# An attention and gated-FFN kernel: its four PSUM pairs addressed as eight banks, and a new written order

## The chip, the core and the metric

The kernel runs on one core of a Trainium2 chip. The metric is the device time of one execution in microseconds (us); lower is better. The kernel before was timed three times: 277.92, 278.68 and 278.79 us, median 278.68 us. Differences of about 0.3% (0.8 us) and more can be told from none.

## What is computed

Block-sparse attention (4 batches, 8 heads, 768 tokens, head size 64), and a gated feed-forward network on its output. The mask lets a block of 32 queries see its neighbour blocks, the first and last block, and three drawn blocks.

```
scores = scale * np.matmul(q, k.transpose(0, 1, 3, 2))
scores = np.where(mask, scores, -1e9);  attn = softmax(scores);  a = attn @ v
x = a.transpose(0, 2, 1, 3).reshape(3072, 512)
gate = 1 / (1 + exp(-(x @ w_gate)));  out = (gate * (x @ w_val)) @ w_out        # d_ff = 1536
```

Inputs and output are float32; the kernel computes in float16 with float32 accumulation.

## The kernel before

**Tiling.** The 3072 tokens are cut into twelve units of 256 queries, three per batch (n = 0 to 11). A unit has four pairs of heads (p = 0 to 3). For each pair there are three steps (j = 0 to 2) of 256 keys: a step's score matmuls (qk) fill a [128, 1024] float32 result in PSUM, ACT takes the exponential into SBUF as float16 (exp), and DVE multiplies it by the 0/1 mask (mul; unit 0 has the mask added in the score matmuls instead, as a bias). Then the value product (pv), its normalisation on DVE (norm: a reciprocal and a multiply; from unit 2 on a fold of two partial sums comes first), and a transpose of the result into xT: by TensorE for units 0 and 1 (turn, and a copy), by a transposing DMA after them. The FFN of a unit or of two units then runs over twelve tiles of 128 hidden columns (f0 to f11): gate and value matmuls, tanh on ACT (it stands for the sigmoid), gate on DVE, and the output product y. A job takes two f tiles for a single unit (units 0 to 3), one for two units.

**Start.** The first heads come in float32 by the hardware queues. All else is loaded by POOL's queue, with a cast to float16, in the order of `FIRST`: k, q for the first unit by pairs (k1 q1 k2 q2 k3 q3), v0 to v3, then the rest of q by pairs (r0 to r3) between the weight tiles w0 to w5 (two f tiles each), then the output weights. K and q of batch 0 are transposed by TensorE (prep); later batches by DMA.

**PSUM.** All of PSUM is four tiles of two banks each, `m0` to `m3` (line 317). Every job takes one such pair whole, also those that need one bank or less: turn, the transposes of prep, the mask tiles, the value product of units 0 and 1.

**The written order.** Each job is a task with a number (`Plan.add`, line 133). The string `ORDER` names the tasks in the order in which they are issued, with the engine (D for DVE, A for ACT) where there is a choice, the pair after a colon, and after an @ a task that must be done before a load goes out. `Plan.run` (line 137) walks the string and calls the tasks. Each engine has one queue and takes its instructions in that order; where an instruction reads or overwrites what another engine's instruction, named earlier in the string, wrote or read, the tile layer adds a semaphore wait to it. A waiting instruction holds everything behind it on its engine.

**Junk.** Tokens that begin with j issue matmuls on zeros into a pair, in front of the first real work on TensorE.

Of the kernel before, what the change touches and what calls it, by code (L numbers as in the profile page):

```python
# [22 lines left out]
NT = S // 128  # L23
# [8 lines left out]
PE, ACT, DVE, DMA, SP = "PADGS"  # L32
# [4 lines left out]
EARLY = 2  # L37
# [3 lines left out]
j3 j3 j3 j3 j3 j3 j3 j3 5A 8D j3 0 11A j3s 9:0 j3s j3s j3s 10D j3s j3s 12:1 1:2 j3s 13A 3:0 2 j3s 34:1 4D 35 15:2  # L41
j3s 32:3 16D 6:0 33 17:1 7D 117:2 18D 97:0 118D 44:1 98A j3s 22:3 78:2 23D 45 36:0 79D 20:3 37 21D
40:2 25:1 30:3 41 26D 76:0 77D 46:1 31 54:2 19 74:0 47 75D 27:3 24 55 50:0 28D 80:1 64:3 51 81D
48:2 65 60:1 49 56:0 61 14 66:3 58:2 67D 105@30 57 29 89:3 59 38:1 90 52:0 86:2 53D 87 39 68:3
93:0 69D 62:1 108:2 94 42:3 109 43D 102:0 63D 111:3 70:1 103 110 126:2 71D 112 104 95:0 84:1 96D
122:3 85A 113 140:0 127 123 91 130:1 128 132:3 141 129 131 72:2 119:0 99:1 73D 133 120 147:2 134
100 135 142 157:0 148 154:3 171:1 124 155 149 158 88 164:3 143:2 156 176:0 92@164 144 121 146@111
101 172 170@44 165 173 161:2 217@54 145 190:1 177 189@46 162 125@40 178 237@54 159 186:3 191 150:2
115:0 151D 192 174:2 187 116 204:1 175 188 231:0 179:3 183:2 232 205 180D 244:3 184 233 206 166
245 82:0 200:2 218 83D 201 246 234:3 193:0 219 194A 152 235 185 153 211:2 136:0 220 137D 212 138  # L50
272:3 195 139 229 223A 202 167:0 255:2 168 236 273 213 221A 239 214:0 230 307:1 274 169 215 275
256 240 216 197:3 308 257 196 181 198 258 248:0 309 182 199 241:2 249 242 310 268:3 262 225:1 250
260 114@268 263 269 251 252:2 226 318:0 261 207:3 319 253 315:1 208 289:2 316 160@315 254 106:0
265:3 243 290 107A 247@265 266 270 276:1 209 291 300:0 293:3 277 301 278 282:1 294 292 283 297 163
303:0 335:2 295 302 222 304 279 227 285:1 336 296 286 238 359:0 305 337 360 210 284 331:3 228
362:1 348 332 361 264 349 363 333 328:0 287 350 329 267 322:3 351A 320 344:1 353A 311:0 323
203@344 345 341:2 387:3 321@359 312 342 317 271@282 426:1 373:0 313 411@300 427 330 397:2 374 398
343 388 346 375 259 408:1 376 389 355:2 400@268 409 390 347@30 419:0 356 334@89 380:3 405:1 428
370:2 381 306@111 364 420 288@44 406 371 386@214 366:3 421 410 365@265 454:2 422 433:1 455 432@380
# [3 lines left out]
442 474:1 484:0 463A 378 465A 339 467:2 452 340 475 524:3 480 485 525 514 354 515:1 327 468 486  # L63
# [4 lines left out]
538 583 438 550:1 567 571 542 439 586 551 638:0 563:2 572 425 539 564 552 595:1 573A 404 577:2 604  # L68
639 574 596 578 609:0 568 597 555 575A 627:2 598 616:3 610 628 617 543@616 635:1 565 712@200 630:2
611 569@300 636 612 592:3 446@563 688:0 631 593 658@60 689 654 706:1 556@231 588:3 707 579 641@550  # L70
640 642:0 632 676@471 619:1 633 589 587@282 620 594 691@214 623:2 690 613 590 670:1 591 643 671
637 605:3 624 644 621 606 645 659:1 618 625 709:0 681:3 710 626 660 607 655:2 682 692:0 656 453
663:3 711 726@99 661 657 608@234 673:2 693 662 674 622@652 664 672 694 548 699:1 695 665 723:2 666
# [3 lines left out]
762 669 782 730:3 745A 734:0 760 757:2 731 735 753 798:3 703 758 799 732 736 764:0 759 750 743A  # L77
600 765 797 826:3 823:1 767 763 824 650 816:0 766 651 827 809:1 756 768 810 719 800 787:3 817 769
733 788 806:1 801:0 807 770D 819:3 789 772A 811 737:1 790:2 839 738 614 802 580 615 791 803 601
# [5 lines left out]
904 856 925 936:0 978:1 913 937 911 857 919:3 979 908 875:0 920 914 876 929:1 921 917A 905 932  # L85
970:3 930 935 971 877 922 946:0 915A 1024:3 931 947 893 1025 928 1027:2 1012:0 939 938 916 1013
948 959:3 1028 966 1040:0 940 960 1041 1026 941 967:2 973:3 944A 942D 968 945 1029 952:0 1001:1
# [6 lines left out]
1078 1074 1094 1008 1082 1095 1083 1084 1100:1 1087A 1096A 1108:3 1088 1098A 1101 1085A 1099 1097  # L94
# [3 lines left out]
1163:2 1154D 1164 1159 1156D 1155 1157 1165 1160 1166 1167 1168:0 1161 1169 1170 1162 1171 1172  # L98
"""
GAP, PV_HALF, PV_PARTS, F_HALF, Y_ONE = 0.3, 0.36, 0.74, 0.875, 0.216  # L100
# [14 lines left out]
class Bank:  # L115


    def __init__(self):
        self.slot = None


class Plan:
# [14 lines left out]
    def run(self):  # L137
        done = set()
        for token in self.order:
            if token[0] == "j":  # L140
                self.idle(int(token[1]), token[2:])
                continue
            i, eng, slot, gate = re.fullmatch(r"(\d+)([PADGS]?)(?::(\d))?(?:@(\d+))?", token).groups()
            i = int(i)
            engines, fn, deps, more = self.tasks[i]
            assert i not in done and done.issuperset(deps)
            done.add(i)
            if slot is not None:
                more["take"].slot = int(slot)
# [7 lines left out]
def kernel(  # L157
# [161 lines left out]
    def both(bank):  # L319
        return units_ps[bank.slot]  # L320

    def both16(bank):
        return units_ps[bank.slot].bitcast(f16)

    def idle(unit, kind):
        n = 1 if kind == "s" else 4
        for i in range(2):
            rows = slice(i * D, (i + 1) * D)
            nc.tensor.matmul(
                units_ps[unit][:, i, 0 : n * 128].rearrange("a (x n) -> a x n", n=128),  # L330
                junk[rows],
# [103 lines left out]

    def mask_tiles(c0, c1, j):

        bank = Bank()

        def mm(eng):  # L440
            for i in range(2):
# [716 lines left out]
```

## Time and profile before

| what | us |
|---|---|
| median of three runs | 278.68 |
| span of the profiled execution | 277.8 |
| PE busy in it | 270.0 |
| DVE busy | 207.1 |
| ACT busy | 192.1 |

The profile shows one execution. PE is TensorE's matmul stream, PEld its weight loads, DVE the vector, ACT the scalar engine, POOL and SP issue DMAs. In the groups of instructions, a row gives the line, the engine, the operation, output and inputs with their shapes, the count, the busy time and the mean of one in ns; after the second bar stands the engine's idle time just before, with what ended it. The timeline gives start and length in us, and in brackets the idle time before. Nearly all matmuls have line 352, a helper's, and so are told apart by their tiles: `qT,kT` the scores, `vex,P` the value product, `xT,wg` and `xT,wv` the FFN's first part, `wo,ht` its second.

### The profile page before, as it was taken

Reading aid. Unit: us, or ns where it says so; the run is one execution under the profiler, and the core shown is the slowest. Engines: PE = TensorE matmul, PEld = TensorE weight load, DVE = VectorE, ACT = ScalarE, POOL = GpSimd, SP = SyncE. Lnnn points to the kernel's source line nnn. Section 1 sums busy time; section 2 is a strip of 40 time slices with the busy share of each in tenths; the row PEclk is TensorE's granted clock in tenths of the full one; section 3 lists DMA queues with packets and bytes.
Section 4 is the critical chain, followed back from the end, with each engine's and each line's share of the span. In section 5 each row is a group of like instructions: output and inputs, shape, how many; then the busy total and the mean of one; then the engine's idle time right before and its main releaser. Section 6 shows DMA issues by size and latency. Waiting matters only on the chain.

```text
span 277.8 us, 11169 instructions
## 1 busy us (share of the span) xinstructions
PE 270.0 (97%) x5007; PEld 178.7 (64%) x5007; DVE 207.1 (75%) x421; ACT 192.1 (69%) x243; POOL 47.3 (17%) x69
## 2 busy tenths in 40 slices
PE   8879999999999999999999999999999999999995
PEld 3667785896897798655566655655655676555543
DVE  4667788899999989978988886887876899004422
ACT  3988868899989958968868965679688571035300
POOL 7776261030480000028300000000000000000000
PEclk9999999999999999999999999999999999999999
DMA  7999999994599693339986743014130002230004
GB/s 160 175 195 197 200 205 198 140 139 100 84 160 145 117 140 97 103 98 167 142 113 113 73 61 97 2 21 142 24 96 4 4 2 76 70 151 2 0 2 151
DMA packets 56684, 28.93 MB, mean 104 GB/s; under 512 B 33036, under 2 KB 53692, under 8 KB 56636
## 3 DMA queue, kind: packets, MB, share of 16 engines
q0 software_dynamic: 21520, 13.90, 35.7%
q1 hardware_dynamic: 34628, 14.02, 24.8%
q8 instruction: 39, 0.64, 1.0%
q10 hardware_dynamic: 488, 0.30, 0.3%
q14 instruction: 9, 0.07, 0.1%
HBM read 28.47 MB, written 6.29 MB: 125 GB/s over the span
## 4 chain that ended last, share of the span: by engine, by line
PE 87%; DMA 7%; POOL 2%; ACT 1%; DVE 1%; issue 1%; SPq 0%
PE m L352 86%; DMA q<-in_q_dram 3%; DMA v<-in_v_dram 2%; DMA kT<-kp 1%; ACT P L586 1%; POOL k L226 1%; POOL q L226 1%; POOL wg L236 0%; POOL wv L236 0%; DVE ysb L888 0%; DVE P L592 0%; ACT ysb L886 0%; PE m L472 0%; PE m L467 0%; ACT ysb L929 0%
## 5 line engine op out<-in xcount | busy, mean ns | idle before, releaser
L586 ACT ACTIVATE P<-m 128x1024 f16<-128x1024 f32 x144 | 143.1, 1025 | 27.8 <-PE m L352 24.6
L352 PE MATMUL m<-xT,wg 64*128 64x512 f16 (+2 forms) x720 | 136.7, 326 | 0.1
L352 PE MATMUL m<-xT,wv 64*128 64x512 f16 (+2 forms) x720 | 136.7, 326 | 0.0
L592 DVE TENSOR_TENSOR P<-P,mask 128x1024 f16<-128x1024 f16 x132 | 87.0, 684 | 2.7 <-ACT P L586 2.6
L352 PEld LDWEIGHTS <-wg 64*128 64x128 f16 (+1 forms) x720 | 66.6, 94 | 21.2 <-issue 0.8
L352 PEld LDWEIGHTS <-wv 64*128 64x128 f16 (+1 forms) x720 | 66.4, 94 | 18.2 <-issue 0.5
L804 DVE SCALAR_TENSOR_TENSOR ht<-th,m 128x512 f16<-128x512 f32 x72 | 49.0, 685 | 37.0 <-ACT th L801 36.1
L352 PE MATMUL m<-wo,ht 64*128 64x512 f16 (+2 forms) x564 | 70.4, 372 | 0.0
L801 ACT ACTIVATE th<-m 128x512 f32<-128x512 f32 x72 | 42.8, 598 | 29.6 <-PE m L352 26.1
L352 PE MATMUL m<-qT,kT 64*128 64x256 f16 x576 | 53.6, 269 | 0.9 <-DMA kT<-kp 0.5
L352 PEld LDWEIGHTS <-P 64*128 64x128 f16 (+1 forms) x2112 | 41.1, 94 | 5.2 <-issue 0.4
L352 PEld LDWEIGHTS <-ht 64*128 64x128 f16 (+1 forms) x564 | 29.4, 94 | 23.4 <-issue 1.3
L352 PE MATMUL m<-vex,P 64*128 64x65 f16 (+1 forms) x2112 | 42.5, 190 | 0.0
L352 PEld LDWEIGHTS <-kT 64*128 64x128 f16 x576 | 26.7, 94 | 17.8 <-issue 1.3
L646 DVE TENSOR_REDUCE acc<-m 128x260 f32<-128x520 f32 x40 | 27.8, 697 | 7.9 <-PE m L352 6.8
L226 POOL DMA_DIRECT2D k<-in_k_dram x15 | 11.1, 744 | 48.3 <-PE m L352 45.0
L886 ACT ACTIVATE ysb<-m 128x512 f32<-128x512 f32 x18 | 10.2, 601 | 11.8 <-PE m L352 11.8
L656 DVE TENSOR_TENSOR x<-acc,rz 128x256 f16<-128x256 f32 x40 | 17.0, 425 | 1.4
L226 POOL DMA_DIRECT2D v<-in_v_dram x16 | 11.6, 736 | 33.5 <-PE m L352 12.9
L226 POOL DMA_DIRECT2D q<-in_q_dram x19 | 13.9, 733 | 3.9 <-DMA wo<-in_moe_w_out_dram 1.8
L352 PE MATMUL m<-bias,e 64*128 64x256 f16 x48 | 5.9, 271 | 2.3 <-DVE mask L299 1.9
L929 ACT ACTIVATE ysb<-m 128x256 f32<-128x256 f32 x1 | 0.4, 383 | 10.1 <-PE m L352 10.1
(47 smaller groups left out, 84.1 us busy)
## 6 DMA issues: line engine op xcount, KB each, us to landing
out_dram<-ysb SPq DMA_DIRECT2D x23, 256.0 KB, 2.4
v<-in_v_dram POOLq DMA_DIRECT2D x16, 192.0 KB, 5.1
k<-in_k_dram POOLq DMA_DIRECT2D x15, 192.0 KB, 6.6
q<-in_q_dram POOLq DMA_DIRECT2D x12, 192.0 KB, 6.4
wg<-in_moe_w_gate_dram POOLq DMA_DIRECT2D x6, 256.0 KB, 8.4
wv<-in_moe_w_val_dram POOLq DMA_DIRECT2D x6, 256.0 KB, 9.0
wo<-in_moe_w_out_dram POOLq DMA_DIRECT2D x3, 512.0 KB, 12.8
xT<-x SPq DMA_TRANSPOSE x40, 2.4
```

Source lines behind the costliest of these rows:

```text
L226: return nc.gpsimd.dma_start(dst[:, h0:h1, t0:t1, :], src[b, h0:h1].rearrange("h (p t) d -> p h t d", t=NT)[:, :, t0:t1, :],)
L352: return nc.tensor.matmul(out, lhsT, rhs, start=start, stop=stop, skip_group_check=True).ins
L586: nc.scalar.activation(self.pt.rearrange("a h i n -> a (h i n)"), both(self.bank).rearrange("a h n -> a (h n)"), AF.Exp, bias=0.0, scale=SCALE
L592: nc.vector.tensor_tensor(self.pt, self.pt, m.unsqueeze(1).broadcast_to([128, 2, 2, UQ]), op=ALU.mult,)
L646: nc.vector.tensor_reduce(self.acc.rearrange("a h s d -> a (h s d)"), self.parts.rearrange("a r n -> a n r"), axis=mybir.AxisListType.X, o ...
L656: nc.vector.tensor_tensor(self.x16.rearrange("a s h d -> a h s d"), self.acc[:, :, :, 0:D], rz.broadcast_to([128, 2, 2, D]), op=ALU.mult,)
L801: nc.scalar.activation(th, both(bank)[:, 0, :], AF.Tanh, bias=0.0, scale=0.5)
L804: nc.vector.scalar_tensor_tensor(self.ht[:, tiles[0] : tiles[-1] + 1, :], in0=th.rearrange("a (f n) -> a f n", n=self.w), scalar=1.0, in1= ...
L886: nc.scalar.activation(ysb, both(bank)[:, s, :], AF.Copy, bias=0.0, scale=0.5)
L929: nc.scalar.activation(ysb, src, AF.Copy, bias=0.0, scale=0.5)
```

## The change

- The four PSUM tiles stay as they are. A job may now be named with a letter a to h instead of a digit: a and b are the two banks of `m0`, c and d of `m1`, e and f of `m2`, g and h of `m3`. `one` gives the half of the tile.
- A job on one bank uses whole columns of 128 rows where the pair form used two row halves in two banks: transposes against the full identity, both mask tiles from one row half, the value product of units 0 and 1 in one accumulation of 4 x 65 columns.
- The FFN of units 0 and 1 (`SMALL = 2`) is done by the new `f1`: one f tile per job, gate in the first 256 columns of a bank and value in the others, a tanh and a gate of 256 columns each. There are 24 such jobs in place of 12. For the first four of unit 0 (`EARLY = 4`; before, the first two jobs, also four f tiles) the part that needs the last pair's xT is a task of its own.
- Junk goes into one bank with all 128 rows.
- `ORDER` is new throughout, with other task numbers, slots, engines and gates. `FIRST` is unchanged. The planner's costs, written at the tasks, are new too; they only matter to whoever makes the order, not to the program.

```diff
+    @property
+    def single(self):
+        return self.slot in "abcdefgh"
...
     units_ps = [ps.tile([128, 2, 512], f32, name=f"m{i}") for i in range(4)]
 
     def both(bank):
-        return units_ps[bank.slot]
+        return units_ps[int(bank.slot)]
...
+    def one(bank):
+        i = "abcdefgh".index(bank.slot)
+        return units_ps[i // 2][:, i % 2, :]
...
+    rings["th1"] = [t[:, c : c + UQ] for t in rings["th"] for c in (0, UQ)]
...
+            if bank.single:
+                if flat:
+                    nc.tensor.transpose(one16(bank)[:, i * 128 : (i + 1) * 128], tile_, ident)
+                    continue
...
+        def f1(self, f):
...
+                    for c in cs:
+                        for g in range(2):
+                            bank.last = tiled(
+                                one(bank)[:, g * UQ : (g + 1) * UQ],
+                                (wg, wv)[g][:, c, f * 128 : (f + 1) * 128],
+                                self.x[:, c, :],
+                                c == 0 and g == 0,
+                                c == 3 and g == 1,
+                            )
...
+            def tanh(eng):
+                nc.scalar.activation(th, one(bank)[:, 0:UQ], AF.Tanh, bias=0.0, scale=0.5)
...
         def f(self, j):
 
+            if self.g < SMALL:
+                for f in range(self.per * j, self.per * (j + 1)):
+                    self.f1(f)
+                return
```

The stretch of the new `ORDER` where the FFN of unit 0 begins (tasks told here by what they do: 136 and 137 f2 in its two parts, 138 its tanh, 139 its gate; 140 and 141 f3, 142 and 143 tanh and gate; 132 and 133 tanh and gate of f1; 70, 72 transposes of q; 111, 119, 148, 122 scores of unit 1 and 112, 120, 149, 123 their exps; 115 and 134 value products of pairs 0 and 1 of unit 1, 116 and 135 their norms; 82 and 83 a mask tile and its copy; 158, 159, 160 f5, its tanh and gate; 155, 156 f4 and its tanh; 113, 121, 150 multiplies by the mask):

```
136:f 137 154@108 138 139 140:c 132 133 141 70:3 142 111:0 143 71A 115:d 82:2 112 119:3 206@119 83
237@119 116 113 158:c 120 159 160 72:2 73 148:0 149 121 150 122:3 123 155:d 156 134:c
```

More of the change, by code (lines that the diff above doesn't have):

```diff
@@ L31 @@
 NU = S // UQ
-PE, ACT, DVE, DMA, SP = "PADGS"
+PE, ACT, DVE, DMA, SP, ONE = "PADGSQ"
 VB = 5
@@ L319, in both, with one16, idle @@
     def both(bank):
-        return units_ps[bank.slot]
+        return units_ps[int(bank.slot)]
     def both16(bank):
-        return units_ps[bank.slot].bitcast(f16)
-    def idle(unit, kind):
-        n = 1 if kind == "s" else 4
[L327 to L331, printed above, removed]
-                junk[rows].unsqueeze(1).broadcast_to([D, n, 128]),
-                start=True,
-                stop=True,
-            )
+        return units_ps[int(bank.slot)].bitcast(f16)
+    def one(bank):
+        i = "abcdefgh".index(bank.slot)
+        return units_ps[i // 2][:, i % 2, :]
+    def one16(bank):
+        i = "abcdefgh".index(bank.slot)
+        return units_ps[i // 2].bitcast(f16)[:, i % 2, :]
+    def idle(at, kind):
+        n = 1 if kind == "s" else 4
+        i = "abcdefgh".index(at)
+        nc.tensor.matmul(
+            units_ps[i // 2][:, i % 2, 0 : n * 128].rearrange("a (x n) -> a x n", n=128),
+            junk,
+            junk.unsqueeze(1).broadcast_to([128, n, 128]),
+            start=True,
+            stop=True,
+        )
     def wait_for(ins, earlier, reason):
@@ L429 @@
         ),
-        [(DVE, 0.42)],
+        [(DVE, 0.335)],
     )
     t_rows = [
-        rows(S, lambda eng, spread: copy(eng, mb24, spread), [(DVE, 0.95), (ACT, 0.82)])
+        rows(S, lambda eng, spread: copy(eng, mb24, spread), [(DVE, 0.87), (ACT, 0.70)])
     ]
@@ L438, in mask_tiles, with half @@
         bank = Bank()
+        w = c1 - c0
+        def half(i):
+            return one(bank)[:, i * w : (i + 1) * w] if bank.single else both(bank)[:, i, 0:w]
         def mm(eng):
@@ L548, in go @@
             )
-        a = plan.add([(DVE, 0.4)], go, deps + read.get(("pv", b - 2, p), []))
+        a = plan.add([(DVE, 0.268)], go, deps + read.get(("pv", b - 2, p), []), needs=(f"v{p}",) if b == 0 else ())
         copies.setdefault(("v", b, p), []).append(a)
@@ L611, in pv @@
         def pv(self, eng):
-            acc = both(self.bank)[:, :, 0 : 2 * (D + 1)]
-            self.acc = acc.rearrange("a h (s d) -> a h s d", s=2)
-            mms = []
+            self.acc = one(self.bank)[:, 0 : 4 * (D + 1)].rearrange(
+                "a (h s d) -> a h s d", h=2, s=2
+            )
             for s in range(2):
                 for t in range(NT):
-                    mms.append(
-                        lambda a, rows, s=s, t=t: (
+                    for a in range(2):
+                        tiled(
                             self.acc[:, a, s, :],
-                            self.steps[t // 2].pt[rows, a, t % 2, s * 128 : (s + 1) * 128],
-                            vex[self.b % 2][rows, 2 * self.p + a, t, 0 : D + 1],
-                        )
-                    )
-            whole(mms, self.bank)
+                            self.steps[t // 2].pt[:, a, t % 2, s * 128 : (s + 1) * 128],
+                            vex[self.b % 2][:, 2 * self.p + a, t, 0 : D + 1],
+                            (s, t, a) == (0, 0, 0),
+                            (s, t, a) == (1, NT - 1, 1),
+                        )
         def pv_parts(self, eng):
@@ L664, in turn @@
             x16 = self.x16.rearrange("a s h d -> a s (h d)")
-            halves(both16(self.bank2), [x16[:, s, :] for s in range(2)])
+            turned_in(self.bank2, [x16[:, s, :] for s in range(2)])
         def evac(self, eng):
@@ L692, in value @@
                 a, free = plan.add(
-                    [(DVE, 0.66)], self.fold, [a] + folded[-3:-2], free=self.bank
+                    [(DVE, 0.609)], self.fold, [a] + folded[-3:-2], free=self.bank
                 ), None
             self.normed = plan.add(
-                [(DVE, 0.6 if free else 0.5)], self.norm, [a] + before("x16", self.i), free=free
+                [(DVE, 0.55)], self.norm, [a] + before("x16", self.i), free=free
             )
@@ L722, in xt @@
                 plan.add(
-                    [(DVE, 0.29), (ACT, 0.37)],
+                    [(DVE, 0.203), (ACT, 0.268)],
                     self.evac,
@@ L748, in scores @@
             take=run[0][1].bank,
-            ops=16 if first else 8,
+            score=True,
+            needs=("e0", "e1") if first else (),
         )
@@ L753, in scores @@
             e = plan.add(
-                [(ACT, 0.98)], st.exp, [a] + before("P", 3 * pr.i + st.j), free=st.bank
+                [(ACT, 0.903)], st.exp, [a] + before("P", 3 * pr.i + st.j), free=st.bank
             )
@@ L844, in f @@
                     take=bank,
-                    lag=GAP,
-                    ops=16 * self.per,
+                    needs=wneeds,
                 )
                 a = plan.add(
-                    [(PE, F_HALF)], half(False), [a], ops=16 * self.per
+                    [(PE, 0.863 if self.w == 512 else 0.872)], half(False), [a], turn=True
                 )
             used["xT"][self.g].append(a)
-            c = plan.add([(ACT, 0.57)], tanh, [a] + before("th", i), free=bank, part=1)
-            g = plan.add([(DVE, 0.68)], gate, [c], free=bank, part=1)
+            old = before("th", i)
+            if i < len(rings["th"]) and used["th1"]:
+                old = [x for m in (2 * i, 2 * i + 1) for x in used["th1"][max(k for k in used["th1"] if k % 6 == m)]]
+            c = plan.add([(ACT, 0.477)], tanh, [a] + old, free=bank)
+            g = plan.add([(DVE, 0.598)], gate, [c], free=bank)
             used["th"][i] = [g]
@@ L898, in part @@
                     take=bank if first and f0 == 0 else None,
-                    lag=0.0 if f0 < 8 else GAP if first else None,
-                    ops=16,
+                    turn=not first and f0 == 0,
+                    needs=(f"o{f0 // 4}",),
                 )
@@ L958, in go @@
                             tiled(
-                                both(bank)[:, 0, 0 : c1 - c0],
+                                one(bank)[:, 0 : c1 - c0],
                                 self.ht[:, f, i * UQ + s * 128 : i * UQ + (s + 1) * 128],
```

275 lines of the change are left out of this document (152 added, 123 removed), and 55 rows, old and new, of the table ORDER.

## The prediction

> **What bounds the kernel now.** First the page: the span, the share of PE, its row of slices, and the chain that ended last.
>
> ```profile
> span 277.8 us, 11169 instructions
> PE 270.0 (97%) x5007; PEld 178.7 (64%) x5007; DVE 207.1 (75%) x421; ACT 192.1 (69%) x243; POOL 47.3 (17%) x69
> PE   8879999999999999999999999999999999999995
> PE 87%; DMA 7%; POOL 2%; ACT 1%; DVE 1%; issue 1%; SPq 0%
> ```
>
> PE sets the end. Then the busy time by stage (columns: stretch and its length, then PE, PEld, DVE, ACT, POOL, granted clock, DMA share, GB/s).
>
> ```profile
> 0.00:10.00 10.00, 8.62 (x139) 4.75 (x143) 5.63 (x17) 5.71 (x8) 8.23 (x16) 1.00 0.98 165
> 10.00:20.00 10.00, 7.90 (x206) 6.28 (x205) 6.46 (x16) 8.84 (x11) 6.64 (x10) 1.00 1.35 187
> 20.00:30.00 10.00, 9.42 (x197) 7.23 (x194) 7.01 (x19) 8.06 (x10) 6.59 (x9) 1.00 1.46 198
> 30.00:80.00 50.00, 50.00 (x1065) 39.70 (x1065) 44.17 (x89) 43.66 (x55) 13.83 (x20) 1.00 1.01 151
> 120.00:130.00 10.00, 9.47 (x181) 5.58 (x178) 7.95 (x16) 6.93 (x9) 6.52 (x10) 1.00 0.76 127
> 130.00:270.00 140.00, 139.88 (x2268) 80.95 (x2264) 96.79 (x186) 84.29 (x112) 2.81 (x4) 1.00 0.32 62
> ```
>
> From 30 us on PE is full: 50.00 of 50, later 139.88 of 140. So from there a stall of PE adds itself to the end, one to one, and only the start (about 4 us idle before 30, 0.53 near 122) has anything to win. The chain of waits in order of time shows those two places (start, length, what):
>
> ```profile
> 13.56 0.77 POOL wg L236
> ...
> 15.57 8.08 DMA q<-in_q_dram
> ...
> 23.69 0.32 PE m L472 x16
> 24.01 1.42 PE m L352 x12
> ...
> 118.66 4.07 DMA kT<-kp
> 122.73 0.05 issue
> ```
>
> The FFN begins at 24 us, when weights and xT are there; the second is a key transpose that came late.
>
> The timeline of the start shows what holds PE there beside data: a write that waits for the reader of its PSUM pair.
>
> ```profile
> 6.73 1.94 ACT L586 ACTIVATE P<-m 128x1024 f16<-128x1024 f32 x2 [0.86 <-PE m L352]
> ...
> 14.35 0.36 DVE L545 COPY vex<-v 128x768 f16<-128x768 f16 x1 [1.53 <-DMA v<-in_v_dram]
> 14.63 0.68 DVE L299 CAST mask<-m 128x512 f16<-128x512 f32 x1
> 15.36 0.29 PE L352 MATMUL m<-bias,e 64*128 64x256 f16 x2 [1.91 <-DVE mask L299]
> 16.01 4.82 ACT L586 ACTIVATE P<-m 128x1024 f16<-128x1024 f32 x5 [1.15 <-PE m L352]
> 22.85 0.61 PE L352 MATMUL m<-qT,kT 64*128 64x256 f16 x8 [0.29 <-DVE x L656]
> 25.84 1.28 DVE L592 TENSOR_TENSOR P<-P,mask 128x1024 f16<-128x1024 f16 x2
> ```
>
> PE stood 1.91 us for a mask copy, because that copy stood on DVE behind a copy of v that waited for its DMA; ACT then stood 1.15 us. The other case cost 0.29. These two rows bound one such wait.
>
> **The change part by part.** The durations, from the groups by form:
>
> ```profile
> L586 ACT ACTIVATE P<-m 128x1024 f16<-128x1024 f32 x144 | 143.1, 1025 | 27.8 <-PE m L352 24.6 <-PE m L467 1.7 <-ACT P L586 0.3
> L801 ACT ACTIVATE th<-m 128x512 f32<-128x512 f32 x72 | 42.8, 598 | 29.6 <-PE m L352 26.1 <-DVE acc L646 2.7 <-DVE ht L804 0.8
> L929 ACT ACTIVATE ysb<-m 128x256 f32<-128x256 f32 x1 | 0.4, 383 | 10.1 <-PE m L352 10.1
> L804 DVE SCALAR_TENSOR_TENSOR ht<-th,m 128x512 f16<-128x512 f32 x72 | 49.0, 685 | 37.0 <-ACT th L801 36.1
> L931 DVE TENSOR_SCALAR ysb<-m 128x256 f32<-128x256 f32 x1 | 0.4, 425 | 1.0 <-PE m L352 1.0
> L655 DVE RECIPROCAL rz<-m 128x4 f32<-128x4 f32 x8 | 1.4, 179 | 0.8 <-PE m L352 0.6
> L656 DVE TENSOR_TENSOR x<-m,rz 128x256 f16<-128x256 f32 x8 | 3.4, 425 | 0.3
> L352 PE MATMUL m<-xT,wg 128*128 128x256 f16 x48 | 10.9, 274 | 0.0
> 29.68 0.28 PE L352 MATMUL m<-xT,wg 128*128 128x256 f16 x1
> 29.80 0.27 PE L352 MATMUL m<-xT,wv 128*128 128x256 f16 x1
> 16.47 0.91 PE L352 MATMUL m<-vex,P 128*128 128x65 f16 x24
> ```
>
> *Work.* An f tile is eight matmuls, one every 0.11 us (29.68 to 29.80): 0.87 us, the same in either form. A tanh or gate of 256 columns is not in the trace; the nearest rows are the 256-column steps on the same engines, 0.38 (L929) and 0.43 (L931); half of 0.60 and 0.69 is the lower end. With 24 for 12, ACT gets 24 x 0.38 - 12 x 0.60 = 1.9 us more, DVE 24 x 0.43 - 12 x 0.69 = 2.0 us. PE's pace by itself hides both (ACT 43.66, DVE 44.17 busy of 50 in that stage); without that cover they lengthen the waits below. One-bank transposes and masks take PE up to twice as long, some 1 us in all, estimated as half of the eleven one-bank jobs' 0.1 to 0.35 us; they fall into the first 24 us, where PE idles more than that.
>
> *The waits.* This decides. The four PSUM tiles are still whole pairs, and in the built program, read with its waits, so are the dependencies: every PE write into one bank of a pair waits also for each reader of the other bank that the order names earlier. Twenty-two PE writes thus wait for a neighbour alone, none of whose data or bank they use: nine up to the start of the FFN, thirteen in the FFN of units 0 and 1. Readers wait likewise for an earlier named PE job in the other bank (the first norm for the second pair's value product). What stands behind such a write is all of PE, and behind PE the next exp. I price the thirteen by laying the order out engine by engine with the rows above. Four of them, in the stretch of the order quoted before:
>
> - 115 (value product, bank d) waits for the gate of f3 in c. Count from the end of the exp that frees the pair for f3. PE: f3 0.9, transposes 0.2, scores 0.2: ready at 1.3. ACT: one exp (0.97 each in a row, 4.82 / 5), three tanhs: done at 2.0. DVE: the multiply of that exp until 1.65 (0.64 each in a row), then three gates: 2.75. Idle 1.4.
> - 158 (f5, c) waits for the norm 116 (d). After the value product PE has a mask matmul and a score, 0.3; DVE copies the mask (0.68), then the norm (0.18 + 0.43): 1.45. Idle 1.15.
> - 155 (f4, d) waits for the gate of f5: tanh and gate 0.85; PE has transposes and two scores, 0.65. Idle 0.2.
> - 134 (value product, c) waits for the tanh of f4, which stands behind two exps: about 1.9 after f4 begins, and f4 takes 0.87. Idle 1.05.
>
> The other nine, laid out the same way: 0.6, 1.3, 0.9, 1.0 in unit 0's FFN; 0.6, 1.3, 2.1, 0, 1.5 in unit 1's. Together 13.0, 1.0 each. By the bounds each is worth 0.29 to 1.91: 3.8 to 24.8 in all. I take 13.0, as the worked ones lie between. Score and value writes into whole pairs right behind these jobs wait for the same readers, four times 0.2 to 0.5, of which the old kernel had some: +1.2.
>
> *The start.* If the pairs cost nothing, the first f tile could go at 20.5: exps of unit 0 end near 19 (twelve at 0.97 from 6.73, one mask copy), a norm and turn later. With the waits on the way (a transpose behind the norm of the next pair, 0.65; a value product behind a copy, 0.35; the f tile behind the last norm, 0.65; an exp late by 1.4) it goes at 23.3 in place of 23.94: -0.6, bounds -1.6 (below, the first rival) and +1.
>
> *The rest.* After unit 1 all jobs but the last take pairs as before, in a new order: nothing to win but the 0.53 near 122: -0.5, bounds -2 (all that PE lost after 30) and +2. The end after the last matmul (a copy, a store) is the same, also the loads up to the output weights.
>
> Sum: 277.8 + 13.0 + 1.2 - 0.6 - 0.5 = 290.9, and the median lies 0.9 above the span: **291.8 us**.
>
> **The rivals.**
>
> 1. *The new order delivers: the readers are done before PE comes to its writes.* For it: 30 to 80 us had ACT and DVE idle 6 us each, and the readers are short (0.38 and 0.43). Then f0 to f5 are done at 30 us, where the old kernel had f0 to f3: 2 x 0.87 = 1.7, and 0.5 near 122: 278.7 - 2.2 = 276.5. It decides if the thirteen waits average under 0.15. Against it: the four worked.
>  The Trainium skill (PSUM — Partial Sum Buffer, Specifications (TRN2)) says that two engines may use PSUM in parallel at full rate as long as they don't meet in a bank. By this the chip would let PE write bank d while c is read, and the outcome would be this rival's; but a semaphore written into the program is obeyed all the same.
> 2. *The waits are half covered.* Where ACT stands idle the tanh comes at once, and a wait is 0.3 to 0.5: 13 x 0.4 = 5.2, with the rest as above: 278.7 + 5.2 + 0.1 = 284.0. For it: rows like the 0.29.
> 3. *The queues jam.* ACT and DVE, 1.9 and 2.0 us fuller, get late; each reader stands behind an exp and a multiply (1.02 + 0.38 + 0.64 + 0.43 = 2.5) half of the time: 1.5 each, 19.5: 298.3. For it: the 1.91 row. Against: each PE stall lets them catch up.
>
> That the change doesn't do what it says, eight banks, is what the forecast itself rests on.
>
> **How the numbers follow.** The forecast (287 to 296) has 0.60, rival 1 0.10, rival 2 0.17, rival 3 0.13. The range of 8 in 10 leaves out rival 1 and the ends of 2 and 3: 282 to 299. Faster by over 0.3% (about what a measurement tells from no change) is rival 1 but for a small rest that ends near nothing: 0.09; same 0.02; slower 0.89.
>
> **What would show it.** Right: in the profile after, PE is no longer full between 24 and 80 us, its busy time there short by over 10 us, and the idle time before line-364 matmuls on `vex,P` and `xT,wg` is ended by DVE `ht`, DVE `x` and ACT `th`, several times by over 1 us; from about 95 us on PE is full again, and unit 2's output store goes out later than before by as much as the end. The first f tile starts near 23. Wrong: PE full from 25 us (rival 1), or the loss found after 100 us, where no job takes a single bank.

## The result, and the profile after

| | median of four, us | lowest to highest |
|---|---|---|
| before | 278.50 | 277.92 to 278.79 |
| after | 316.99 | 315.15 to 318.22 |

The changed kernel takes 1.138 times as long (95% interval 1.1332 to 1.1431): 38.5 us more, where some 13 were forecast. The profiled execution took 318.22 us.

The page of the kernel after: the span, the share of PE, the 40 slices of 7.9 us each for PE and its granted clock, and the chain that ended last.

```profile
span 316.4 us, 10880 instructions
...
PE 282.1 (89%) x4849; PEld 191.6 (61%) x4849; DVE 209.4 (66%) x433; ACT 193.3 (61%) x255; POOL 47.2 (15%) x69
...
PE   8887687987898617999999999999999999999984
...
PEclk9999999999999785999999999999999999999999
...
PE 70%; DMA 9%; DVE 9%; ACT 6%; issue 3%; POOL 3%; DVEq 0%; ACTq 0%
```

PE is not full from 24 to 80 us, as forecast. But there is a second hole, three slices (6, 1, 7) between 103 and 127 us, and in the same slices the clock falls (7, 8, 5). In the windows of the kernel after (columns: stretch and length, then PE, PEld, DVE, ACT, POOL, granted clock, DMA share, GB/s):

```profile
20.00:50.00 30.00, 21.72 (x350) 16.04 (x347) 20.21 (x48) 20.97 (x29) 13.65 (x19) 1.00 1.35 199
50.00:80.00 30.00, 24.56 (x432) 17.17 (x430) 22.08 (x53) 20.19 (x30) 7.74 (x11) 1.00 0.97 144
...
100.00:130.00 30.00, 17.63 (x320) 13.98 (x318) 13.89 (x29) 10.42 (x14) 0.72 (x1) 0.77 0.77 107
```

The last stretch in the kernel before:

```profile
100.00:130.00 30.00, 29.48 (x662) 20.98 (x660) 25.86 (x55) 24.30 (x30) 6.52 (x10) 1.00 0.61 110
```

Between 100 and 130 us PE is busy 11.9 us less. The low clock takes some of the busy time too: in windows of 1 us, PE's busy time times the share of the clock that was missing adds up to 4.5 us. Together that is an estimated 16.4. Between 20 and 80 us PE is busy 46.3 of 60, against 59.4 before: 13.1 less.

**The first loss** is what was forecast. PE's timeline of the kernel after (start, length, what; in brackets the idle time before it and what ended it):

```profile
26.52 0.27 PE L364 MATMUL m<-xT,wg 128*128 128x256 f16 x1 [0.73 <-DMA q<-in_q_dram]
...
34.38 0.89 PE L364 MATMUL m<-vex,P 128*128 128x65 f16 x24 [1.43 <-DVE ht L832]
...
36.82 0.27 PE L364 MATMUL m<-xT,wg 128*128 128x256 f16 x1 [1.12 <-DVE x L690]
...
38.03 0.61 PE L364 MATMUL m<-qT,kT 64*128 64x256 f16 x8
38.31 0.42 DVE L832 SCALAR_TENSOR_TENSOR ht<-th,m 128x256 f16<-128x256 f32 x1 [0.94 <-ACT th L829]
...
38.78 0.27 PE L364 MATMUL m<-xT,wg 128*128 128x256 f16 x1
...
40.73 0.89 PE L364 MATMUL m<-vex,P 128*128 128x65 f16 x24 [0.92 <-ACT th L829]
```

PE's rows at 34.38, 36.82, 38.78 and 40.73 begin tasks 115, 158, 155 and 134; the row at 38.31 is DVE's. Task 155 waits for the gate of f5, which ends at 38.31 + 0.42 = 38.73; PE's scores before it end at 38.64. That leaves 0.14 us, which the timeline does not mark. PE's waits between 23 and 100 us that end with a gate, a tanh or a norm (us in total, times, longest):

```profile
PE m L364 <- DVE ht L832: 7.0, 8, 1.7
PE m L364 <- ACT th L829: 3.2, 4, 1.1
PE m L364 <- DVE x L690: 1.1, 1, 1.1
```

Thirteen, 11.3 us together, 0.87 each. Eleven of them stand in front of writes into single banks, 10.5 us. The other two, 0.38 us at 78.72 and 0.39 at 84.84, stand in front of a score and a value product, which write whole pairs.

**The second loss** was not forecast. DVE's timeline, two neighbouring rows:

```profile
102.94 0.69 DVE L680 TENSOR_REDUCE acc<-m 128x260 f32<-128x520 f32 x1
117.91 0.36 DVE L559 COPY qp<-q 128x768 f16<-128x768 f16 x1 [14.27 <-DMA qT<-qp]
```

A copy of the last batch's queries may overwrite `qp` only when the transpose of batch 2's queries has read it, and that transpose was late. DVE works in order, so masks and gates stood behind the copy, and PE behind these. The transfers issued between 88 and 118 us (KB each, median us from issue to landing), in the kernel after:

```profile
v<-in_v_dram POOLq DMA_DIRECT2D x5, 192.0 KB, 13.6
q<-in_q_dram POOLq DMA_DIRECT2D x4, 192.0 KB, 10.5
k<-in_k_dram POOLq DMA_DIRECT2D x4, 192.0 KB, 7.0
...
xT<-x SPq DMA_TRANSPOSE x3, 6.2
kT<-kp SPq DMA_TRANSPOSE x3, 10.9
qT<-qp SPq DMA_TRANSPOSE x2, 7.9
```

The same stretch before:

```profile
xT<-x SPq DMA_TRANSPOSE x9, 2.9
qT<-qp SPq DMA_TRANSPOSE x4, 2.5
kT<-kp SPq DMA_TRANSPOSE x3, 3.3
```

Before, no load is issued in this stretch. After, thirteen go out beside the transposes, and those of keys and queries take some three times as long. Twelve are the loads of the last batch, which the new order puts behind scores of units 3 and 4 (`588@376`, `673@437` and so on).

PE's idle time in the hole has two pieces: 8.42 us until 120.68, ended by a fold on DVE (`acc`), and 3.95 us until 105.55. Only the first stands behind the copy, for PE goes on at 105.55 while DVE is still waiting. The second falls inside one f tile, after the first of its matmuls, so no wait for a tile fits there. Two kernels below that keep these loads (the copies later; the tail's buffers) stop at the same matmul, for 5.07 and 4.53 us. The page of the kernel after lists one more queue on the DMA engines, `q8 instruction`, with 38 packets and 0.62 MB. Its packets came at 86.1, 95.6 and 102.7 us; in the kernel below with the last batch's transfers moved away they came at 90.5, 96.2, 100.3 and 104.4, and there PE does not stop like this. So PE may have waited for its own instructions, whose transfers were late beside the loads. No run separates this.

**The tail.** PE stands once more ahead of its last 24 products, because an evacuation waits until an older store has left its buffer:

```profile
307.73 0.42 DVE L1016 TENSOR_SCALAR ysb<-m 128x256 f32<-128x256 f32 x1 [4.03 <-DMA out_dram<-ysb]
...
308.21 4.06 PE L364 MATMUL m<-wo,ht 128*128 128x512 f16 x24 [1.23 <-DVE ysb L1016]
```

### The profile page after: what moved, and what is told of

It reads as the page before. It is cut to its first block, busy times and chain, and to the rows that moved or that the text cites. A ratio compares the mean times of both kernels' runs of the same rounds, so it can differ in the third digit from the quotient of the medians.

```text
span 316.4 us, 10880 instructions
## 1 busy us (share of the span) xinstructions
PE 282.1 (89%) x4849; PEld 191.6 (61%) x4849; DVE 209.4 (66%) x433; ACT 193.3 (61%) x255; POOL 47.2 (15%) x69
## 4 chain that ended last, share of the span: by engine, by line
PE 70%; DMA 9%; DVE 9%; ACT 6%; issue 3%; POOL 3%; DVEq 0%; ACTq 0%
PE m L364 70%; ACT P L620 4%; DVE P L626 3%; DMA q<-in_q_dram 3%; DMA qT<-qp 3%; DMA wg<-in_moe_w_gate_dram 2%; DVE ht L832 2%; ACT th L829 2%; DMA out_dram<-ysb 1%; POOL v L231 1%; POOL q L231 1%; DVE acc L680 1%; POOL k L231 1%; DVE ysb L1016 0%; DVE x L690 0%
## 5 line engine op out<-in xcount | busy, mean ns | idle before, releaser
L620 ACT ACTIVATE P<-m 128x1024 f16<-128x1024 f32 x144 | 140.6, 1029 | 38.6 <-PE m L364 37.8
L364 PEld LDWEIGHTS <-wv 64*128 64x128 f16 (+1 forms) x672 | 63.2, 96 | 39.8 <-issue 20.6
L364 PEld LDWEIGHTS <-wg 64*128 64x128 f16 (+1 forms) x672 | 63.5, 96 | 21.2 <-issue 2.5
L903 DVE SCALAR_TENSOR_TENSOR ht<-th,m 128x512 f16<-128x512 f32 x60 | 40.6, 684 | 38.4 <-ACT th L900 38.1
L900 ACT ACTIVATE th<-m 128x512 f32<-128x512 f32 x60 | 35.7, 599 | 47.4 <-PE m L364 45.1
L364 PEld LDWEIGHTS <-ht 64*128 64x128 f16 (+1 forms) x564 | 32.3, 94 | 25.7 <-issue 2.0
L364 PEld LDWEIGHTS <-kT 64*128 64x128 f16 x576 | 29.9, 96 | 12.6 <-issue 3.3
L832 DVE SCALAR_TENSOR_TENSOR ht<-th,m 128x256 f16<-128x256 f32 x24 | 9.7, 418 | 9.5 <-ACT th L829 9.5
L829 ACT ACTIVATE th<-m 128x256 f32<-128x256 f32 x24 | 8.9, 386 | 11.4 <-PE m L364 9.4
L231 POOL DMA_DIRECT2D v<-in_v_dram x16 | 11.5, 718 | 22.8 <-PE m L364 15.4
L559 DVE COPY qp<-q 128x768 f16<-128x768 f16 x12 | 4.2, 358 | 14.3 <-DMA qT<-qp 14.3
```

What stands on the lines that cost most here:

```text
L231: return nc.gpsimd.dma_start(dst[:, h0:h1, t0:t1, :], src[b, h0:h1].rearrange("h (p t) d -> p h t d", t=NT)[:, :, t0:t1, :],)
L364: return nc.tensor.matmul(out, lhsT, rhs, start=start, stop=stop, skip_group_check=True).ins
L559: nc.vector.tensor_copy(dst[:, p, :, :, :], src[:, 2 * p : 2 * p + 2, :, :].rearrange("a h t d -> a t h d"),)
L620: nc.scalar.activation(self.pt.rearrange("a h i n -> a (h i n)"), both(self.bank).rearrange("a h n -> a (h n)"), AF.Exp, bias=0.0, scale=SCALE
L829: nc.scalar.activation(th, one(bank)[:, 0:UQ], AF.Tanh, bias=0.0, scale=0.5)
L832: nc.vector.scalar_tensor_tensor(self.ht[:, f, :], in0=th, scalar=1.0, in1=one(bank)[:, UQ : 2 * UQ], op0=ALU.add, op1=ALU.mult,)
```

## The experiments

Times without a range are single executions; those of the kernel before beside them lay between 278.13 and 280.34 us. The four executions of the kernel after lie 3.1 us apart, so a difference of that size between two single executions shows little.

### Waits by bank

The order stays. Each PSUM instruction loses its waits for users of the other bank of its pair, and gets a wait for the last users of its own:

```diff
-    plan.run()
+    traced = []
+    nc.push_inst_callback(traced.append)
+    plan.run()
+    nc.pop_inst_callback()
...
+        for name, engine, theirs, outs2, reads2 in mine:
+            if meet(outs, outs2 + reads2) or meet(reads, outs2):
+                continue
+            if engine != ins.engine and not theirs & (w | r):
+                tc.declare_no_dep(ins, name, reason="the other bank of the pair")
...
+        for n, name in last.values():
+            tc.add_manual_dep(ins, name, edge, reason="the same bank")
```

> The changed kernel with the same order, but each PSUM instruction's waits on users of the other bank of its pair are taken away (banks are ordered by bank). Theory (two separate losses: some 15 us of waits for the neighbour bank before 80 us, and a pile-up of transfers of some 16 us between 100 and 130 us): the first goes, the second stays and comes some 13 us earlier; DVE still waits over 10 us once for a transposing transfer; 301 to 304 us. Rival A (the pile-up is only a result of the first delay): both go, 284 to 288 us. Rival B (the waits for the neighbour bank do not bind, another wait stands behind them): over 312 us.

It took 305.85 us, 11.1 below after and just above the theory's 301 to 304; both rivals are out. Its windows, and two of its waits between 60 and 150 us (us in total, times, longest):

```profile
20.00:50.00 30.00, 29.24 (x485) 21.56 (x481) 26.61 (x63) 28.46 (x41) 15.78 (x22) 1.00 1.36 201
50.00:80.00 30.00, 22.65 (x377) 16.21 (x378) 20.05 (x50) 16.73 (x26) 7.51 (x12) 0.89 1.29 176
```

```profile
DVE qp L559 <- DMA qT<-qp: 13.4, 1, 13.4
...
PE m L364 <- DMA qT<-qp: 5.9, 1, 5.9
```

From 20 to 50 us PE is as full as before the change (29.24 against 29.42), so the waits for the neighbour were the whole loss of that stretch. The first f tile starts at 23.22. The hole behind the last batch's loads stays, as the theory had it. And a loss appears that had been hidden: PE, now earlier, stands 5.9 us for a transpose of batch 1 that is issued beside value loads of batch 1 and first loads of batch 2.

### The last batch's loads later

```diff
-588@376 673@437 723@458 575@440 690@429 744@429 619@429 654@415 640@415 708@475 601@475 758@489
+690@556 673@582 575@582 640@582 723@559 619@598 588@595 744@572 601@634 758@613 654@585 708@569
```

with the copies and transposes that use them named some 60 to 130 tokens later.

> The changed kernel with the twelve loads of the last batch, the eight copies that use them, their transposes and four copies of V named later (loads behind scores of units 5 and 6 in place of unit 4); nothing else moved. Theory (loads and transposes share the DMA engines, DVE stands for a late transpose): DVE's one wait of 14.3 us for the transposes of qT is gone, transposes between 85 and 120 us land in 3 to 6 us in place of 10 to 13, PE is busy over 18 of 20 us in 100 to 120, 299 to 302 us. Rival (the transposes are late because the whole order is late, not because of the loads): the hole stays in another place, over 311 us.

312.44 us: 4.6 below after, so by the time it falls to the rival (over 311). But the hole was gone from where it had been: PE busy 28.68 of 30 between 100 and 130. Its transfers between 88 and 118 us, and a wait between 80 and 160:

```profile
xT<-x SPq DMA_TRANSPOSE x6, 4.0
kT<-kp SPq DMA_TRANSPOSE x4, 3.4
qT<-qp SPq DMA_TRANSPOSE x3, 3.6
```

```profile
DVE x L689 <- DMA xT<-x: 5.1, 1, 5.1
```

The new wait comes from this kernel's own order: it names the eight transposes on SP in front of older xT transposes, whose buffers the norms need. Between 140 and 160 us PE was busy 13.45 of 20, at a clock of 0.83: some 9 us lost. The kernel after the next does without this wait.

### The copies later, the loads left

> The changed kernel with the eight copies of the last batch's keys and queries, their transposes and the four copies of V named later, as in the run with later loads, but the twelve loads left where they are. Theory (the loss comes through one link, the copy on DVE that waits for a late transpose, and the scores of unit 6 need the late transposes only after 130 us): transposes still take 10 to 13 us, DVE's wait of 14.3 us is gone, 299 to 304 us. Rival (late transposes hold PE by themselves, through scores or xT): at most 5 us less, over 311 us.

317.9 us, which is the rival's range. The wait of 14.3 us on DVE is gone, the transposes still take 11.0 us, and between 100 and 130 PE is busy 24.93 of 30; but the jam on SP is in this kernel too. That the copy is not the only link is what can be said: PE stood 5.1 us there with no late copy, in the stop inside an f tile that was told of above. That a late transpose held it is not shown.

### The last batch alone, with SP's order mended

```diff
-588@376 673@437 723@458 575@440 690@429 744@429 619@429 654@415 640@415 708@475 601@475 758@489
+640@527 619@582 588@582 575@559 723@595 744@572 690@613 673@585 654@569 601@648 758@670 708@637
```

and the transposes behind the old xT transposes. Nothing of batches 1 and 2 moves.

> The changed kernel with only the last batch's loads, copies and transposes later and wider, and its transposes behind the old xT transposes on SP (in the run x2_loads they went in front of these and jammed SP in turn). PSUM waits by pair, batches 1 and 2 untouched. Theory (the hole between 100 and 130 us costs some 16 us against before by itself): the hole is gone, no stretch of 10 us after 90 us loses more than 3 us, 301 to 304 us. Rival (the work behind the hole is bound elsewhere too, so that only some 5 us come back, as in x2_loads): 309 us or more.

301.54 us: 15.4 below after, as the theory had it. The stretch of the hole:

```profile
100.00:130.00 30.00, 29.61 (x737) 26.72 (x734) 27.59 (x53) 24.24 (x31) 6.44 (x9) 1.00 0.71 101
```

The granted clock is back at 1.00. This is the second loss, measured by itself; loads, copies and transposes moved together.

### Early loads in the kernel before

The other way round: the kernel before, with six loads of the last batch moved and nothing else.

```diff
-543@616 658@60 556@231 641@550 587@282 608@234
+658@481 543@481 556@481 587@481 641@474 608@474
```

> The kernel before, untouched but for six of the last batch's loads of keys and queries, which go out behind scores near 92 us, beside the transposes of batch 2, in place of 123 to 138 us; nothing else is named elsewhere. Theory (loads in flight slow the transposes, whatever the kernel): the median of the six transposes of keys and queries issued between 90 and 106 us goes from 2.6 us to 5 us or more, while the time changes little, 277 to 282 us, because in this order no copy waits for them. Rival (transposes are slow in the changed kernel for another reason): they land as before, in under 4.5 us.

289.14 us, 10.8 more than the 278.34 of the kernel before beside it; the transposes behaved as expected, the time did not. Its transfers between 88 and 106 us, one row of PE, and PE's waits between 80 and 150 us:

```profile
q<-in_q_dram POOLq DMA_DIRECT2D x3, 192.0 KB, 11.0
k<-in_k_dram POOLq DMA_DIRECT2D x3, 192.0 KB, 12.2
...
qT<-qp SPq DMA_TRANSPOSE x3, 12.6
...
kT<-kp SPq DMA_TRANSPOSE x2, 7.0
```

```profile
102.61 0.56 PE L352 MATMUL m<-vex,P 64*128 64x65 f16 x13 [4.88 <-issue]
```

```profile
PE m L352 <- issue: 6.7, 2, 4.9
...
PE m L352 <- DMA kT<-kp: 1.0, 1, 1.0
```

No bank is single here. So the loss comes with where the loads stand, not with the banks, and needs no copy behind a late transpose. The two stops of 6.7 us, the 1.0 us for a transpose and an estimated 2.7 us by the low clock (windows of 1 us, as above) are 10.4 of the 10.8. So the transposes were slow, but little of the loss is a wait for them. What released PE after 4.88 us the profile does not show. The stop falls inside one value product, after 35 of its 48 matmuls, and the packets of `q8 instruction` came at 88.1 and 99.8 us, where the kernel before has 89.2, 94.5 and 99.0. As above, instructions that came late beside the loads would fit; this is argued and not shown.

### Both together

Waits by bank with the first version of the later loads:

> Waits by bank and later loads together. Theory (separate losses that add): 285 to 289 us, which leaves the tail (2 us) and some 6 us not placed. Rival (they overlap, each hides part of the other): over 293 us. If the new order does what it was made for: 276 to 280 us.

301.03 us, in the rival's range: it has the jam on SP and the batch 1 loss of the two kernels it is made of. With the mended version:

> Waits by bank (11.1 us by themselves) and the last batch's transfers later (15.4 us by themselves) together, batches 1 and 2 as in the changed kernel. Theory (two losses that add, each measured where the other does not hide it): 286 to 290.5 us, that is 26.5 to 31 us below the changed kernel, and what is left lies between 50 and 80 us, where the run with waits by bank alone lost 10 us to the transfers of batch 1. Rival (they overlap): 292 us or more.

291.97 us (291.63 to 292.31, four executions; ratio to before 1.0494, interval 1.0451 to 1.0537), 25.0 below after, where the two alone gave 11.1 + 15.4 = 26.5. They add but for 1.5. The theory's 286 to 290.5 is missed by that much, and the time lies at the edge of the rival's 292. What is left, in its windows and in PE's timeline:

```profile
50.00:80.00 30.00, 21.58 (x406) 16.04 (x404) 18.78 (x47) 17.20 (x26) 7.26 (x11) 0.83 1.28 175
```

```profile
61.04 1.03 PE L363 MATMUL m<-qT,kT 64*128 64x256 f16 x8 [8.28 <-DMA qT<-qp]
```

One wait for a transpose of batch 1, and a low clock until 66 us. Most of the low clock falls into the wait itself; in windows of 1 us it costs the busy time an estimated 2.2 us. With the 8.4 us idle that is 10.6 of the 13.8 us by which this kernel is behind the one before.

### Spreading the other transfers

Four kernels moved loads, copies and transposes of batches 1 and 2 as well. In the first two the value loads of batch 1 and the first three loads of batch 2 went behind most of batch 1's transposes:

```diff
-171@165 114@220 267@220 223@203 314@231 295@231 366@231
+171@231 114@231 267@231 223@292 314@308 295@308 366@308
```

> The changed kernel, PSUM waits by pair as in it, with transfers spaced: the value loads of batch 1 and the first three loads of batch 2 behind the transposes of batch 1; the loads of batch 3 as in the run with later loads; the transposes of batch 3 later than there, behind the old xT transposes. Theory (waits for the neighbour bank cost some 9 us before 50 us, and most of the 9 us lost between 50 and 90 us are also theirs; the rest was transfers): 100 to 160 us is full but for 2 us, 296 to 300 us. Rival (between 50 and 90 us the transfers bind too): 289 to 293 us.

> Waits by bank, transfers spaced as in the run beside it, and the last three output tiles in buffers of their own. Theory (bank waits, crowded transfers and the tail are all that was lost): 276 to 282 us, PE full from 20 us on. Rival (a third cause in the order, such as DVE or ACT late between 50 and 80 us): over 286 us, with PE short of full between 50 and 80 us and no transpose above 7 us there.

311.88 us by pair and 295.62 by bank (the tail's buffers with it): both missed their theories. The gates still let the loads go at 46 and 58 us, and the 50 to 80 us stretch of the second had PE busy 21.69 of 30, with a wait of 5.5 us for `kT`; the third cause that its rival named was not found, and its transposes landed there after 6.0 to 8.9 us at the median, where that rival had none above 7. Then all three batches wider, by bank and by pair, both with the tail's buffers. Of the loads:

```diff
-171@165 114@220 267@220 223@203 314@231 295@231 366@231 353@308 443@308 464@308 397@330 418@289
+171@292 114@292 267@308 223@308 314@333 295@289 366@289 353@289 443@350 464@350 397@350 418@391
```

> Waits by bank, the tail's own buffers, and the loads, copies and transposes of batches 1 to 3 all spread: the value loads of batch 1 after the last of its transposes but one, the loads of batch 2 after those and before its copies (which come some 10 us later than in the changed kernel), batch 3 as before but wider apart. Theory (what was left between 50 and 80 us in the last run, 12.5 us, was loads crowding the transposes of batch 1): 281 to 285 us, transposes issued between 45 and 80 us land in under 6 us at the median. Rival (the transposes of batch 1 are late by their own number and order on SP): over 290 us.

> The run beside it with PSUM waits by pair, as in the changed kernel: the two differ in the waits for the neighbour bank alone. Theory (these waits cost what the prediction had for them, 13 to 15 us, wherever no transfer is late): 12 to 16 us above the run beside it. Rival (only 9 to 10 us before 50 us are theirs, the FFN of unit 1 loses none): 8 to 11 us above it.

291.34 and 306.73 us. The first is in its rival's range, though the transposes of queries and keys landed as its theory had it, after 4.2 and 5.9 us at the median. The two differ by 15.4, within the 12 to 16 of the second's theory. Three other pairs of kernels differ in these waits alone, with the transfers of batch 1 left where they were: by 11.1 (the kernel after), 11.4 (the last batch's loads later) and 9.6 us (the same with SP's order mended). So 15.4 is the price of the waits for the neighbour where late transfers hide little of them, between two single executions. By pair, PE has again thirteen waits for `ht`, `th` and `x` between 23 and 100 us (7.3 + 3.2 + 1.1 us); by bank it has none of these, so all thirteen were for a neighbour, and its two longest are for transposes:

```profile
PE m L363 <- DMA kT<-kp: 3.2, 1, 3.2
PE m L363 <- DMA qT<-qp: 0.8, 1, 0.8
```

The last try put the loads of batches 1 and 2 another 5 to 10 us later:

```diff
-171@292 114@292 267@308 223@308 314@333 295@289 366@289 353@289 443@350 464@350 397@350 418@391
+171@308 114@394 267@330 223@289 314@347 295@350 366@350 353@350 443@391 464@311 397@426 418@373
```

> As the run with waits by bank and spread transfers (291.3 us), with the value loads of batch 1 and all loads of batch 2 some 5 to 10 us later still, so that the transposes of batch 1 go out alone, one of these transposes named before an xT transpose that waits, and batch 3 wider. Theory (the 6 us lost between 60 and 70 us there were transfers): that stretch loses under 2 us, 284 to 288 us. Rival (PE waits there for copies on DVE, or the loss moves to batch 2 again): 290 us or more.

290.55 us (289.69 to 291.33, ratio 1.0414, interval 1.037 to 1.0459), with the same wait of 3.2 us for `kT`: the rival. Value loads of batch 1 still went out beside the last of its transposes, at 55 to 60 us; whether these hold them or their own place on SP was not separated. None of these kernels beats the one before.

### The tail's buffers

```diff
-            ysb = home("ysb", 2 * n + s)
+            ysb = self.last_home(s)
```

where `last_home` is a free buffer of the exps.

> The changed kernel with the last three output tiles evacuated into buffers of their own in place of the ring of four, nothing else. Theory (the first of these evacuations waits for a store to land, and PE for it): PE's idle time of 1.2 us before the last 24 products is gone, 314 to 315.5 us. Rival (the wait only moves to the last bank or the last store): 316 to 317.5 us.

```profile
306.59 4.06 PE L364 MATMUL m<-wo,ht 128*128 128x512 f16 x24 [0.51 <-DVE P L1016]
```

The wait shrank from 1.23 to 0.51; the time, 316.58 us, lies in the rival's range and within that of the kernel after. So the tail's 0.7 us can't be told from no change.

## Why the prediction was wrong

The direction was right, and so was the mechanism that carried it; the time lies 18 us beyond the range, because a second loss of the same size had no term.

- **The waits, 13.0 + 1.2.** The mechanism is right, and the sum by some luck. The four that were worked out at 1.4, 1.15, 0.2 and 1.05 measured 1.43, 1.12, 0.14 and 0.92. The closeness of the first two is in part luck: 1.65 and three gates of the 0.43 beside it are 2.94 and not 2.75, and 0.68 + 0.18 + 0.43 is 1.29 and not 1.45, so by its own rows the prediction had 1.6 and 1.0. The other nine came to 0.23, 0.98, 0.62 and 0.76 in unit 0's FFN and 0.53, 1.11, 1.67, none and 1.14 in unit 1's, 7.0 against 9.3. The thirteen together are 10.6 against 13.0, and the two waits into whole pairs 0.8 against 1.2. Rivals 2 and 3, with 0.4 and 1.5 a wait, are further off. PE's busy time between 24 and 80 us is short by 12.4, "over 10", and its idle rows are ended by `ht`, `x` and `th`.
- **The start, -0.6.** Off: the first f tile came at 26.52 in place of 23.3. The seven kernels with waits by pair have it at 24.5 to 26.6, the six with waits by bank at 21.0 to 24.1. So the price of the waits on the way, 23.3 - 20.5 = 2.8, was near (the medians lie 2.6 apart), and the 20.5 to which it was added was too early. The 15.4 us by which two kernels differ hold these waits as well; the forecast had 13.0 + 1.2 + 2.8 = 17.0 for all of them.
- **The rest, -0.5 with bounds of 2.** This step failed. "After unit 1 all jobs but the last take pairs as before, in a new order" looked at PSUM alone. The new order also moves twelve loads from 123 to 138 us to 88 to 101 us, into the transposes of batch 2, and 15.4 us came back when they, their copies and their transposes went later. Of the hole, 8.42 us of PE's idle time stand behind one late transpose; what ended the other 3.95 stays open. The bound of -2, "all that PE lost after 30", is 0.65 in its own rows, 0.53 and 0.12. The step "also the loads up to the output weights" stopped exactly where the loads begin to differ. The kernel before, given six of these loads early, lost 10.8 us: the price could not be read from its profile, but that no load stands beside its transposes of batch 2 could, and from the new order that this ends: reason enough for a wider bound than 2.
- **"From about 95 us on PE is full again."** Wrong for that reason, from 100 to 130 us, and "the loss found after 100 us" was named as what would prove the forecast wrong. It holds for all after 130 but the tail.
- **The end the same.** Off by little: one wait of 1.23 us.
- **Rival 1 and the rule beside it** (the Trainium skill, PSUM — Partial Sum Buffer, Specifications (TRN2): ScalarE and VectorE use PSUM in parallel at full rate as long as they don't meet in a bank). The trace of the kernel with waits by bank agrees: between 23 and 50 us an exp takes 1.035 us (1.027 in the kernel after), a gate 0.414 (0.417) and PE's f matmuls 0.27 in both, while PE writes beside the banks that ACT and DVE read. What that rival lacked was what the forecast lacked: even with its mechanism granted, the time was 305.85 us and not 276.5.

The account of the 38.5 us: 25.0 go when both losses are taken away. Of the 13.8 left against the kernel before in that comparison, 10.6 are one wait for a transpose of batch 1 and the low clock with it; that loads make this transpose late is likely (PE's waits for transposes of that batch fell from 8.3 to 4.0 us when loads were spread) but was not separated from its place on SP. The other 3 are not placed, and which part of the loss between 50 and 80 us in the changed kernel is already this transpose was not separated.

## What to carry to other kernels

A buffer cut in two is only worth something if the dependencies are cut too: look in the built program which semaphore a write waits for, and price the waits engine by engine; that came here within 0.45 us of each wait and high by 2.4 of 13.0 in the sum. When an order is made anew, lay its transfers beside the old ones over the whole run, not only where the edit is: ask what is in flight on the DMA engines whenever a transfer that somebody waits for is issued, and look also for stops that no tile explains. A loss that is measured by taking it away shows only what the next one leaves of it (9.6 to 11.4 of 15.4 us here), so measure it again where the next is gone too.

## What the hardware showed beside

- **Loads slow a transpose, here two to five times.** A transpose of keys or queries lands after 2.5 to 3.3 us at the median with no load issued beside it (the kernel before, 88 to 118 us), and after 7.0 to 12.6 in the two kernels that issue six or thirteen loads there. Other stretches show less: between 45 and 80 us the kernel after has 5.6 and 5.9 us, with thirteen loads. Its issue is slow as well: SP took 5.27 us for the transpose at 99.43 in the kernel after, 1.27 for the one at 91.57 in the kernel before. The Trainium skill (DMA: Bandwidth & Descriptors, Queues, rings and completion order) says that a DMA engine takes its queues in turn, a packet at a time. That fits, but no run here shows the turns.
- **The half clock after a wait.** After 3.95 us of idle time the matmuls of the kernel after came at half pace for some 3.4 us:

```profile
105.55 0.28 PE L364 MATMUL m<-xT,wv 64*128 64x256 f16 x1 [3.95 <-issue]
...
106.29 0.42 PE L364 MATMUL m<-xT,wv 64*128 64x256 f16 x1
...
106.50 0.42 PE L364 MATMUL m<-xT,wv 64*128 64x256 f16 x1
...
109.41 0.27 PE L364 MATMUL m<-xT,wv 64*128 64x256 f16 x1
...
109.52 0.27 PE L364 MATMUL m<-xT,wv 64*128 64x256 f16 x1
```

 One of this form every 0.21 us, later every 0.11. The Trainium skill (TensorE: Matmul & The Clock Gate, Part 1: The HAM clock gate) has it that an idle window of about 3.4 us halves the clock, and as long a busy one restores it. This stop agrees with it. Two others do not fit so well. In the stop of 8.42 us the clock falls after some 4 us, but comes back only at 126.4, 5.7 us after PE goes on at 120.68. And in the kernel with the tail's own buffers, whose order is that of the kernel after, PE came at half pace from 35.3 to 38.7 us behind waits of 1.43 and 1.12 with 1.3 us of work between them:

```profile
20.00:50.00 30.00, 22.47 (x338) 16.28 (x334) 18.84 (x44) 19.75 (x28) 13.11 (x18) 0.94 1.35 200
```

 The profiled execution of the kernel after has the same two waits (1.43 and 1.12) with the clock at 1.00. So waits of 1 us may cost the clock or not, and a longer one costs more than itself: an estimated 4.5 us on top of 11.9 in the second hole.
